# Weights loaded in one go, score banks apart in the first segment, and a planner with refitted transfers and a reserve on every engine, in an attention and Fourier kernel

## The chip, the cores and the metric

The kernel runs on one core of one Trainium2 chip. The core has TensorE (PE in the profile: matmuls; PEld: its weight loads), VectorE (DVE), ScalarE (ACT), GpSimd (POOL) and SyncE (SP), which here issues all the DMAs. The metric is the device time of one launch in microseconds. Three runs of the kernel before took 1836.32, 1828.71 and 1827.49 us; the median is 1828.71.

## The reference

Four layers on x of 2048 rows by 512: attention with a compressive memory (A), a two-dimensional Fourier transform (B), and both again with the same weights. Each is added to its input, after a layer norm.

```python
def _A_ref(x, wq, wk, wv, wo, beta):          # 32 heads of 16, N=4 segments of L=512
    q, k, v = heads(x @ wq), heads(x @ wk), heads(x @ wv)
    phi = lambda t: jnp.where(t > 0, t + 1.0, jnp.exp(t))
    for s in range(N):
        logits = einsum("bhqd,bhkd->bhqk", qs, ks) * scale + mask     # causal
        a_dot = einsum("bhqk,bhkd->bhqd", softmax(logits), vs)
        a_mem = einsum("bhld,bhde->bhle", phi(qs), M) / (einsum("bhld,bhd->bhl", phi(qs), z) + 1e-6)
        outs.append(g * a_mem + (1.0 - g) * a_dot)                    # g = sigmoid(beta)
        M = M + einsum("bhld,bhle->bhde", phi(ks), vs)
        z = z + phi(ks).sum(rows)
    return concat(outs) @ wo
def _B_ref(x, ...):                            # real part of the 2D transform
    a, b = x @ dft_hid_re.T, x @ dft_hid_im.T
    return dft_seq_re @ a - dft_seq_im @ b
x = x + _A_ref(_layernorm(x), ...); x = x + _B_ref(_layernorm(x), ...)   # and both once more
```

## The kernel before

Float32 products are made of float16 halves: every operand is scaled by a power of two and split into a high and a low half (`split`, L367), and three matmuls (`mm3`, L324) make one product.

**Streams.** The work is written as sixteen generators (L1071) and short tasks (`spawn`, L321). Each yields what it needs next: an engine, the tiles that it reads, and the kinds of buffers that it takes. The loop at L1079 asks the planner (`Plan`, L40) when each could go, takes the one with the earliest time, and lets it issue its next instructions. So the order of the instructions on each engine is fixed when the program is built, by the planner's estimates; at run time each engine works its list in that order, and waits where an operand is late. `Plan.op` (L135) holds the estimates: a duration for each operation, a latency after it (`LAT`, L43), and for a DMA the issue and a tail (L171 to L175, or an `est` at the call). `RESERVE` (L35) makes the loop count data that POOL or a DMA wrote as ready 500 or 1000 ns later, for TensorE alone (L132).

**Attention.** A segment of 512 rows has four groups of eight heads (eight segments in two layers, so 32 groups, numbered from 0). For each group: projections of q and k (`s_p`, L682; 24 matmuls, `b<-g,w` in the profile) and v (`s_v`, L707; 48, `b<-w,g`); the halves go through DRAM (`d`) into `qst` and `kst` (`t_split`, L584), of which there are two each (`NR`), so that group i+2 is loaded when the second pass of group i is done. A first pass of scores (`s_x`, L777; 32 matmuls `b<-kst,qst`) serves only to find each row's maximum: DVE adds the causal mask and reduces (`t_max`, `junk<-b,cmask`), the maxima are transposed on PE (`b<-identf,mx`) and written into two rows of `qst` by DMA. A second pass (`s_st`, L827; 32 matmuls `b<-qst,kst`) gives the transposed scores with the maximum taken off; ACT takes the exponential, POOL masks (`t_sel`, L816), and `s_av` (L849) multiplies with v (`b<-w,vt`). `s_mem` (L730) keeps the memory (`b<-vt,w` and `b<-w,macc`). `t_merge` (L548) divides, with the reciprocal of the sums going through DRAM and back.

**After it.** `s_o` (L904) multiplies with wo (`b<-wo,w`), `t_res` adds and takes the layer norm, `s_ab` (L1010) multiplies with the hidden transform (`b<-wd,w`), and `s_f` (L1041) with the sequence transform (`b<-w,w`, 3072 matmuls in 14 chunks), whose blocks are loaded raw, scaled and split once (`s_r`, `s_c`) and kept in DRAM for the second layer.

**Weights.** At the start (L273 to L285) the four tiles of x and the blocks of wq and wk for group 0 are loaded. `s_w` (L376) takes the largest magnitude of each block (`absmax`), finds the scale (`scales`, L348: a transpose on PE, a reduction, and a matmul with ones that spreads it), splits the block and stores it to DRAM for the later segments. After group 0's blocks it waits for the four layer norms, then loads the other ten blocks and `beta`, takes the scale of wv over all four blocks, and goes on group by group. `s_wo` (L415) does the same with wo and the hidden transform.

**Buffers.** Eight banks of PSUM (L255) are shared among four kinds, each with a number kept for it and a most: `pj` for projections and the like, `av`, `dft`, and `ss` for both passes of scores.

Of the kernel before, what the change touches and what calls it, by code (L numbers as in the profile page):

```python
# [31 lines left out]
SLACK = 0  # L32
# [7 lines left out]
class Plan:  # L40


    LAT = dict(T=197.0, V=150.0, A=165.0, G=100.0, Y=0.0)  # L43

    def __init__(self):
        self.free = dict.fromkeys("VGATYD", 0.0)
        self.acc = {}
        self.cols = {}
        self.wr = {}
        self.rd = {}  # L50
        self.area, self.count, self.slot = {}, {}, {}
        self.fresh = set()
        self.fine = {}
        self.by = {}
        self.dma = None
        self.mode, self.units, self.begun, self.entered = "m", {}, 0.0, 0.0
# [67 lines left out]
    def ready(self, reads, tags, eng):  # L124
# [3 lines left out]
        for t in reads:  # L128
# [3 lines left out]
            r = max(r, self.wr.get(n, 0.0) + (RESERVE.get(self.by.get(n), 0.0) if eng == "T" else 0.0))  # L132
        return r

    def op(self, eng, name, args, kw):  # L135
# [7 lines left out]
        if eng == "T":  # L143
            n, w = out[0].free_size(), aps[1]
            slow = 4 if w.dtype == F32 else 1
            c = n / 2.4 * slow + (18 if w.dtype == F32R else 3)
            cols = n * slow * w.partition_size() / 128
            mode, unit = "m", 0
            if name == "matmul" and out[0].partition_size() == 32:
                mode, unit = "v", out[0].start_partition() // 32  # L150
            elif w.partition_size() <= 64:
                mode, unit = "h", w.start_partition() // 64
        elif eng == "A":
# [11 lines left out]
        elif eng == "G":  # L165
            c = 127 + n * 0.915 if name == "affine_select" else 96 + n * 2.2
# [4 lines left out]
        else:  # L171
            stored = out[0].space == bass.MemoryType.DRAM
            c, tail = self.dma or (440, 350 if stored else 950)
            if kw.get("transpose"):
                c, tail = 1350, 450  # L175
# [25 lines left out]
        if eng == "T":  # L201
            self.begun = t
            self.units[unit] = e
            if len(self.units) < dict(m=1, h=2, v=4)[mode]:
# [39 lines left out]
def body(ctx: ExitStack, tc: tile.TileContext, x, wq, wk, wv, wo, beta, wd, cs, out):  # L244
# [10 lines left out]
    pl.setup(psum, "b", 8, dict(pj=(1, 4), av=(2, 2), dft=(1, 2), ss=(2, 4)))  # L255
    pl.setup(work, "w", NW, dict(
        xi=(4, 6), hl=(1, 4), qhl=(1, 3), phm=(2, 3), phr=(1, 2), mu=(1, 1), kt=(1, 2), pn=(1, 2), md=(2, 2), mz=(1, 1),
        en=(1, 1), wt=(2, 3), wv=(1, 2), craw=(4, 8), cc=(4, 8), pt=(8, 12), ot=(4, 8), xb=(2, 4),
# [26 lines left out]
    load(0, 1)  # L285
    macc = const.tile([128, NG, 2, 4, 32], F32, name="macc")
# [34 lines left out]
    def spawn(g):  # L321
        tasks.append([next(g, None), g])
# [8 lines left out]
    mk = const.tile([128, 1], F32, name="mk")  # L331
    V.memset(mk, 0.0)
# [15 lines left out]
    def scales(a, b):  # L348
        k = b - a
        yield need("T", amax[:, b - 1:b], tag="ss")  # L350
        pm = ps("ss")
        T.transpose(pm[0:k, 0:128], amax[:, a:b], identf)
        yield need("V", pm)
        V.tensor_reduce(mk[0:k], pm[0:k, 0:128], axis=AX.X, op=OP.max)
        V.tensor_scalar(mk[0:k], mk[0:k], 1e-30, None, op0=OP.max)
        dg = rg("dg", 3, F32, (128, 4))
        V.tensor_scalar(dg[:, 0:k], identf[:, 0:k], mk, None, op0=OP.mult)
        yield need("T", dg)
        T.matmul(pm[:, 256:256 + k], ones, dg[:, 0:k], start=True, stop=True)
        yield need("V", pm)  # L360
        gi, si, vi = (t[:, a:b].bitcast(I32) for t in (gmax, scl, inv))
        V.tensor_scalar(gi, pm[:, 256:256 + k].bitcast(I32), 0x7F800000, None, op0=OP.bitwise_and)
        pl.close(pm)
# [8 lines left out]

    def flat(t):
        return t.rearrange("p a b -> p (a b)")

    def s_w():  # L376
        def part(n, g):
# [3 lines left out]
            yield from split(w, stage[g][n], scl[:, i:i + 1])  # L381
# [5 lines left out]
        for g in range(NG):  # L387
            for n in range(2):
                yield need("V", stage[g][n])
                absmax(2 * g + n, flat(stage[g][n]))  # L390
            yield from scales(2 * g, 2 * g + 2)
            for f, n, e in ((f_q, 0, -10), (f_k, 1, -10), (f_k2, 1, 12)):
                V.tensor_scalar(f[g], inv[:, 2 * g + n:2 * g + n + 1], 2.0 ** e, None, op0=OP.mult)
            V.tensor_scalar(f_s[g], inv[:, 2 * g:2 * g + 1], inv[:, 2 * g + 1:2 * g + 2], 2.0 ** 22,
# [769 lines left out]
```

## Time and profile before

| | |
|---|---|
| median of three runs | 1828.71 us |
| span of the profiled execution | 1824.8 us |
| TensorE busy | 1697.8 us, 93% |
| VectorE busy | 1085.9 us, 60% |
| ScalarE busy | 897.1 us, 49% |
| GpSimd busy | 724.6 us, 40% |
| mean granted TensorE clock | 0.971 |
| DMA | 242.44 MB, 133 GB/s |

The page gives the span of the profiled execution, from its first instruction to its last; its time with what lies around the span isn't given apart from the runs, whose median is 3.9 us over the span. "Busy" leaves out waits. A row of the timeline has its start, its length, engine, line, operation, tiles written and read (buffer numbers left out), shapes and count, and in brackets the idle time ahead of it with what ended it. Since nearly all instructions are issued in one helper, they carry its line, L237, and are told apart by their tiles.

### The profile page before, as it was taken

How to read it: one execution, taken by the hardware profiler on the slowest of the kernel's cores; microseconds unless marked ns; L12 is line 12 of the kernel's file. 1: busy time of each engine (PE TensorE's matmuls, PEld its weight loads, DVE VectorE, ACT ScalarE, POOL GpSimd, SP SyncE). 2: the span in 40 equal slices, each digit the busy share in tenths (PEclk: the TensorE clock that was granted, in tenths of full speed). 3: DMA queues.
4: the chain of work that ended last, by engine and by line, in shares of the span. 5: the costliest groups of instructions: out<-in, count | busy, mean ns of one | idle time of the engine just before them, and what ended most of it. 6: DMA issues, size and time to landing. Idle time of an engine off the chain costs nothing. (4 is left out here: it accounts for less than half of the span.)

```text
span 1824.8 us, 32643 instructions
## 1 busy us (share of the span) xinstructions
PE 1697.8 (93%) x11045; PEld 742.2 (41%) x11045; DVE 1085.9 (60%) x3404; ACT 897.1 (49%) x1563; POOL 724.6 (40%) x1158
## 2 busy tenths in 40 slices
PE   3878799989989999999999879999999999999999
PEld 2433334443433434344444333434444434444444
DVE  7786955577765877565556655564656567533211
ACT  2557656757465666644436655555445444431000
POOL 3234545546363464553434543442534334231000
PEclk8988899999999999999999898999999999999999
DMA  7345535655454653345784541553544444222233
GB/s 190 105 135 132 170 74 165 156 152 150 127 147 136 191 149 102 119 151 167 232 226 156 136 124 49 144 131 100 132 110 114 141 120 102 83 84 81 93 122 115
DMA packets 240985, 242.44 MB, mean 133 GB/s; under 512 B 129777, under 2 KB 152305, under 8 KB 240817
## 3 DMA queue, kind: packets, MB, share of 16 engines
q1 hardware_dynamic: 240816, 240.35, 46.9%
q8 instruction: 87, 1.43, 0.3%
q14 instruction: 82, 0.66, 0.1%
HBM read 152.96 MB, written 63.70 MB: 119 GB/s over the span
## 5 line engine op out<-in xcount | busy, mean ns | idle before, releaser
L237 PEld LDWEIGHTS <-w 128*128 128x128 f16 x4992 | 463.8, 98 | 613.3 <-issue 113.0
L237 PE MATMUL b<-w,w 128*128 128x512 f16 x3072 | 708.9, 380 | 2.0 <-ACT w L237 1.7
L237 POOL TENSOR_TENSOR w<-w,w 128x512 f16<-128x512 f32 (+1 forms) x316 | 380.6, 1208 | 412.6 <-ACT w L237 266.9
L237 ACT ACTIVATE w<-b,fac 128x512 f32<-128x512 f32 (+1 forms) x728 | 420.9, 658 | 176.6 <-PE b L237 156.0
L237 DVE CUSTOM_DVE_ANT_0 junk<-b,cmask 128x128 bf16<-128x128 f32 (+3 forms) x1024 | 437.6, 485 | 77.7 <-PE b L237 76.3
L237 POOL TENSOR_SCALAR_AFFINE_SELECT w<-w 128x128 f32<-128x128 f32 (+2 forms) x704 | 242.4, 357 | 309.5 <-ACT w L237 302.6
L237 DVE SCALAR_TENSOR_TENSOR y<-b,fyu,y 128x512 f32<-128x512 f32 x200 | 149.2, 746 | 217.7 <-PE b L237 217.2
L237 ACT ACTIVATE w<-b 128x512 f32<-128x512 f32 (+1 forms) x240 | 138.2, 600 | 251.9 <-PE b L237 240.4
L237 ACT ACTIVATE w<-w,csc 128x512 f16<-128x512 f32 (+1 forms) x256 | 181.1, 721 | 60.7 <-DVE csc L237 51.5
L237 PE MATMUL b<-g,w 128*128 128x512 f16 x768 | 190.4, 391 | 7.4 <-DMA g<-w 5.8
L237 PE MATMUL b<-w,vt 128*32 128x512 f32 (+3 forms) x2048 | 186.2, 460 | 3.0 <-POOL w L237 2.2
L237 PE MATMUL b<-wd,w 128*128 128x512 f16 x768 | 178.7, 380 | 0.9 <-DVE w L237 0.5
L237 ACT ACTIVATE w<-w 128x512 f16<-128x512 f32 (+1 forms) x144 | 90.7, 635 | 168.5 <-DVE w L237 117.4
L237 DVE SCALAR_TENSOR_TENSOR w<-b,w 128x512 f16<-128x512 f32 x128 | 88.1, 688 | 132.6 <-ACT w L237 131.9
L237 PE MATMUL b<-kst,qst 62*128 62x128 f16 (+3 forms) x1024 | 131.9, 314 | 25.3 <-DMA kst<-d 10.0
L237 PE MATMUL b<-qst,kst 64*128 64x512 f16 (+3 forms) x1024 | 123.8, 308 | 16.4 <-ACT w L237 6.1
L237 PE MATMUL b<-w,g 128*128 128x128 f16 x1536 | 99.5, 224 | 10.9 <-DVE mx L237 4.8
L237 PEld LDWEIGHTS <-g 128*128 128x128 f16 x1536 | 91.2, 100 | 25.1 <-issue 14.5
L237 PEld LDWEIGHTS b<-w,vt 128*32 128x32 f32 x2048 | 55.9, 111 | 101.0 <-issue 56.4
L237 PEld LDWEIGHTS <-kst 64*128 64x128 f16 x1024 | 38.3, 95 | 137.2 <-issue 124.7
L237 PE MATMUL b<-wo,w 128*128 128x512 f16 x384 | 89.7, 379 | 0.2 <-ACT w L237 0.2
L237 DVE DVE_READ_ACCUMULATOR2_ANT mx<- 128x1 f32 x1024 | 84.5, 83 | 0.0
(102 smaller groups left out, 887.1 us busy)
## 6 DMA issues: line engine op xcount, KB each, us to landing
w<-in_cs_dram SPq DMA_DIRECT2D x128, 256.0 KB
cc<-w SPq DMA_DIRECT2D x128, 256.0 KB
w<-cc SPq DMA_DIRECT2D x128, 256.0 KB
w<-w SPq DMA_DIRECT2D x96, 256.0 KB
d<-w SPq DMA_DIRECT2D x128, 128.0 KB
w<-rec SPq DMA_DIRECT2D x56, 256.0 KB
w<-in_x_dram SPq DMA_DIRECT2D x32, 256.0 KB
qst<-d SPq DMA_DIRECT2D x64, 128.0 KB
```

The lines of the kernel that those rows point to most:

```text
L237: r = f(*args, **kw)
```

## The change

**Loads.** All twelve blocks of wq, wk and wv, and `beta`, are loaded at the start, straight after x. The pools of split blocks may hold up to eight and four.

**Scales.** `scales` is one matmul with ones over the partitions' maxima, so the sum of 128 maxima stands in for the largest, and the scale is smaller by some powers of two. `s_w` takes the scale of group 0's blocks first, then the maxima of all the others and one matmul for seven columns. `share` takes the place of `split` for all blocks but group 0's wq and wk: ACT writes the high half, and then the scaled block in place; POOL or DVE (`tt` chooses) subtracts.

**Banks.** Until the first output projection (`together`) the first pass has banks of the kind `sx`, the second of `st`, two to four each; then both share `ss` as before.

**Planner.** Latencies, the time of small matmuls in float32 and of 32-row ones, POOL's time and all DMA estimates have new values; a DMA has an issue, a time on the queue and a tail, and SP is held while eight are under way. The reserve holds for every engine. The rule that holds back scores while other matmuls are ready now takes in whatever takes a score bank, the transpose of the maxima too. `RANK` is empty, so it only replaces the way to choose among equals.

```diff
-SLACK = 0
+RANK = {}
+APART = dict(pj=(1, 4), av=(1, 2), dft=(0, 2), sx=(2, 4), st=(2, 4), ss=(0, 4))
+SHARED = dict(pj=(1, 4), av=(2, 2), dft=(1, 2), sx=(0, 2), st=(0, 2), ss=(2, 4))
...
-    LAT = dict(T=197.0, V=150.0, A=165.0, G=100.0, Y=0.0)
+    LAT = dict(T=235.0, V=115.0, A=150.0, G=85.0, Y=25.0)
...
-            r = max(r, self.wr.get(n, 0.0) + (RESERVE.get(self.by.get(n), 0.0) if eng == "T" else 0.0))
+            r = max(r, self.wr.get(n, 0.0) + RESERVE.get(self.by.get(n), 0.0))
...
-            c, tail = self.dma or (440, 350 if stored else 950)
+            c, took, tail = self.dma or ((415, 917, 364) if stored else (470, 829, 755))
...
+        if eng == "Y" and len(self.lands) >= 8:
+            t = max(t, self.lands[-8])
...
-            self.free["D"] = max(self.free["D"], e + 650) + out[0].nbytes() / 360
+            self.free["D"] = max(self.free["D"], e + 590) + took
             e = self.free["D"] + tail
+            self.lands.append(e)
...
-    pl.setup(psum, "b", 8, dict(pj=(1, 4), av=(2, 2), dft=(1, 2), ss=(2, 4)))
+    pl.setup(psum, "b", 8, dict(APART))
...
     load(0, 0)
     load(0, 1)
+    Y.dma_start(gb[:, 0, :], beta)
+    for j in range(NG):
+        for n in range(3):
+            if j or n == 2:
+                load(j, n)
...
     def scales(a, b):
         k = b - a
-        yield need("T", amax[:, b - 1:b], tag="ss")
-        pm = ps("ss")
-        T.transpose(pm[0:k, 0:128], amax[:, a:b], identf)
+        yield need("T", amax[:, b - 1:b], tag="dft")
+        pm = ps("dft")
+        T.matmul(pm[:, :k], ones, amax[:, a:b], start=True, stop=True)
         yield need("V", pm)
-        V.tensor_reduce(mk[0:k], pm[0:k, 0:128], axis=AX.X, op=OP.max)
-        V.tensor_scalar(mk[0:k], mk[0:k], 1e-30, None, op0=OP.max)
-        dg = rg("dg", 3, F32, (128, 4))
-        V.tensor_scalar(dg[:, 0:k], identf[:, 0:k], mk, None, op0=OP.mult)
-        yield need("T", dg)
-        T.matmul(pm[:, 256:256 + k], ones, dg[:, 0:k], start=True, stop=True)
-        yield need("V", pm)
+        V.tensor_scalar(gmax[:, a:b], pm[:, :k], 1e-30, None, op0=OP.max)
+        pl.close(pm)
...
+    def share(o, src, s):
+        yield need("A", src, s)
+        A.activation(o[:, 0], src, AF.Copy, scale=s)
+        A.activation(src, src, AF.Copy, scale=s)
+        yield need("VG", o, src)
+        tt(o[:, 1], src, o[:, 0], OP.subtract)
...
+        yield from scales(0, 2)
+        yield from part(0, 0, split)
+        yield from part(1, 0, split)
+        for j in range(1, NG):
             for n in range(2):
+                yield need("V", stage[j][n])
+                absmax(2 * j + n, flat(stage[j][n]))
+        for j in range(NG):
+            yield need("V", stage[j][2])
+            V.tensor_reduce(vm[:, j:j + 1], flat(stage[j][2]), axis=AX.X, op=OP.max,
+                            apply_absolute_value=True)
+        V.tensor_reduce(amax[:, 8:9], vm, axis=AX.X, op=OP.max)
+        yield from scales(2, 9)
+        factors(0, NG)
+        done.add("WL")
+        yield from part(2, 0, share)
+        for g in range(1, NG):
+            for n in range(3):
+                yield from part(n, g, share)
...
+    def together():
+        apart[0] = False
+        kinds.update(SHARED)
...
-                if w[2][:2] == ("ss", "ss") and r + EARLY >= other:
-                    both = pl.ready(w[1], w[2] + ("ss", "ss"), w[0])
+                if w[2][:1] in (("ss",), ("sx",), ("st",)) and r + EARLY >= other:
+                    both = pl.ready(w[1], w[2] + w[2][:2], w[0])
```

**What moves.** SyncE's list near the program's start, before: `y` is where the weights land, `g` the transposed x, `w_128` a block stored to DRAM.

```order
L237 DMA y<-in_wk_dram 128x4x128
L237 DMA_TRANSPOSE g_276<-w_305 128x8x128
L237 DMA_TRANSPOSE g_276<-w_308 128x8x128
L237 DMA_TRANSPOSE g_276<-w_316 128x8x128
L237 DMA_TRANSPOSE g_276<-w_345 128x8x128
L237 DMA w_128<-w_344 128x1024
L237 DMA w_129<-w_354 128x1024
L237 DMA gb<-in_beta_dram 128x4
L237 DMA y<-in_wv_dram 128x4x128 x2
```

The same place on SyncE with the change:

```order
L246 DMA y<-in_wq_dram 128x4x128
L246 DMA y<-in_wk_dram 128x4x128
L246 DMA y<-in_wv_dram 128x4x128
L246 DMA_TRANSPOSE g_285<-w_316 128x8x128
L246 DMA_TRANSPOSE g_285<-w_323 128x8x128
L246 DMA_TRANSPOSE g_285<-w_329 128x8x128
L246 DMA w_137<-w_342 128x1024
L246 DMA w_138<-w_355 128x1024
L246 DMA_TRANSPOSE g_285<-w_350 128x8x128
L246 DMA y<-in_wo_dram 128x4x512
```

The ten loads that stood behind the transposes and the stores stand ahead of them, and the fourth transpose stands behind two stores.

TensorE's list where group 0's first pass ends and its maxima are transposed, before: `w_580` is group 1's block of wq.

```order
L237 MATMUL b_664<-kst_102,qst_104 128x512
L237 LDWEIGHTS qst_104
L237 MATMUL b_665<-kst_102,qst_104 128x512
L237 MATMUL b_675<-identf,mx 32x128
L237 LDWEIGHTS w_580
L237 MATMUL b_683<-g_276,w_580 128x512
```

With the change `w_773` is a block of group 3, and `kst_114` and `qst_116` hold group 1:

```order
L246 MATMUL b_875<-g_285,w_773 128x512
L246 MATMUL b_889<-identf,mx 32x128
L246 LDWEIGHTS w_773
...
L246 LDWEIGHTS qst_116
L246 MATMUL b_912<-kst_114,qst_116 128x128
...
L246 MATMUL b_913<-kst_114,qst_116 128x128
```

Projections of all four groups stand ahead of this place or at it, and group 1's first pass follows at once; before, group 1's projections came here, and its first pass after group 0's second.

TensorE's list at the end of group 1's first pass, with the change; `qst_115` and `kst_113` hold group 0:

```order
L246 MATMUL b_1011<-kst_114,qst_116 128x512
L246 LDWEIGHTS kst_113
L246 MATMUL b_1018<-qst_115,kst_113 128x512
...
L246 MATMUL b_1026<-qst_115,kst_113 128x512
L246 LDWEIGHTS qst_116
L246 MATMUL b_1031<-kst_114,qst_116 128x512
```

Group 0's second pass stands between the pairs of group 1's first, in banks of its own.

More of the change, by code (lines that the diff above doesn't have):

```diff
@@ L1112, in body @@
         if ready:
-            first = min(r for r, _ in ready)
-            best = next(q for q in ready if q[0] <= first + SLACK)
+            best = min(ready, key=lambda q: (q[0], q[1][2]))
         if best is None:
```

110 lines of the change are left out of this document (52 added, 58 removed).

## The prediction

> **What bounds the kernel now.** I read the page first, for the engine that is nearest to full, then the windows, to see in which stretches it is not full, then TensorE's timeline at the start.
>
> ```profile
> span 1824.8 us, 32643 instructions
> PE 1697.8 (93%) x11045; PEld 742.2 (41%) x11045; DVE 1085.9 (60%) x3404; ACT 897.1 (49%) x1563; POOL 724.6 (40%) x1158
> PE   3878799989989999999999879999999999999999
> PEclk8988899999999999999999898999999999999999
> ```
>
> TensorE (PE) is busy 93% of the span, no other engine over 60%. The slices show where the rest lies: the first six or so, and a dip about slice 23. So an edit can only win PE's idle time, 1824.8 - 1697.8 = 127.0 us, and what a lowered clock costs beside it.
>
> ```profile
> 0.00:266.00 266.00, 201.25 (x1421) 88.08 (x1423) 202.31 (x718) 136.98 (x243) 98.99 (x181) 0.88 0.49 136
> 266.00:1000.00 734.00, 707.39 (x4555) 315.49 (x4552) 472.02 (x1392) 433.70 (x730) 361.11 (x503) 0.99 0.55 157
> 1000.00:1110.00 110.00, 91.79 (x692) 36.72 (x692) 69.84 (x274) 63.78 (x116) 46.38 (x98) 0.86 0.47 126
> 1110.00:1825.00 715.00, 697.37 (x4382) 301.95 (x4378) 341.69 (x1022) 262.67 (x474) 218.08 (x377) 1.00 0.39 108
> ```
>
> The columns are the stretch, its length, busy time of PE, its weight loads, DVE, ACT and POOL, then the granted PE clock and the DMAs. PE idles 64.8 us in the first 266 us (266.00 - 201.25), at a clock of 0.88; 26.6 in the next 734; 18.2 about the second layer's start; 17.6 in the last 715. I cut at 266 because the first matmul of the sequence transform comes there; from then on PE always has transform work to put between the steps of the attention. What comes before is a chain of steps, and the change works on that chain.
>
> ```profile
> 18.87 8.23 PE L237 MATMUL b<-g,w 128*128 128x512 f16 x24 [5.79 <-DMA g<-w]
> 30.41 0.27 PE L237 MATMUL b<-identf,amax 128*1 128x128 f32 x1 [3.31 <-DVE amax L237]
> 36.54 0.27 PE L237 MATMUL b<-w,g 128*128 128x128 f16 x1 [4.02 <-ACT w L237]
> ...
> 40.98 0.61 PE L237 MATMUL b<-kst,qst 62*128 62x128 f16 x8
> ...
> 55.80 0.39 PE L237 MATMUL b<-identf,mx 128*32 128x128 f32 x1 [3.91 <-DVE mx L237]
> 55.99 4.19 PE L237 MATMUL b<-g,w 128*128 128x512 f16 x12
> ...
> 62.30 0.60 PE L237 MATMUL b<-qst,kst 64*128 64x512 f16 x4
> ...
> 80.73 0.62 PE L237 MATMUL b<-kst,qst 62*128 62x128 f16 x12
> ...
> 96.49 0.40 PE L237 MATMUL b<-identf,mx 128*32 128x128 f32 x1 [1.62 <-DVE mx L237]
> ...
> 128.83 0.28 PE L237 MATMUL b<-identf,mx 128*32 128x128 f32 x1 [2.78 <-DVE mx L237]
> ...
> 162.18 0.27 PE L237 MATMUL b<-identf,mx 128*32 128x128 f32 x1
> ...
> 229.81 3.40 PE L237 MATMUL b<-wo,w 128*128 128x512 f16 x15 [0.15 <-ACT w L237]
> ...
> 266.29 1.90 PE L237 MATMUL b<-w,w 128*128 128x512 f16 x8
> ```
>
> Each row has its start and length, and in brackets the wait and what ended it. Group 0's projections run at 18.87, its scores (kst,qst) at 40.98, the transpose of its maxima (mx) at 55.80, its second pass (qst,kst) at 62.30. Group 1's projections come only now, at 55.99, since its weights were loaded late; so its scores begin at 80.73. Maxima of groups 1, 2 and 3 are transposed at 96.49, 128.83 and 162.18. The output projection (wo) starts at 229.81, the first transform at 266.29.
>
> **The change part by part.** *Weights at once.* All twelve blocks are loaded behind x, so SyncE's queue has 16 loads of 256 KB, 4.19 MB, ahead of the transposes that PE first needs.
>
> ```profile
> 24.00:27.00 3.00, 3.00 (x13) 1.12 (x11) 0.92 (x2) 0.60 (x1) 0.00 (x0) 1.00 1.17 316
> 9.35 7.59 SPq L237 DMA_TRANSPOSE g<-w  x4
> ...
> 21.36 0.51 SPq L237 DMA_DIRECT2D y<-in_wv_dram  x1
> ...
> 32.01 1.94 SPq L237 DMA_DIRECT2D qst<-d  x4
> 33.99 1.81 SPq L237 DMA_DIRECT2D kst<-d  x4
> ```
>
> ```profile
> 26.77 0.69 DVE L237 TENSOR_REDUCE vm<-y 128x1 f32<-128x512 f32 x1 [1.26 <-DMA y<-in_wv_dram]
> ```
>
> At the 316 GB/s of the window 4.19 MB take 13.3 us, so they land at 15 to 18 us. The order then has three transposes, two stores and the fourth transpose. In the trace a load issued at 21.36 behind others was used at 26.77, 5.4 us later, so I count waiting in the queue: projections at 22.5 and not 18.87, +3.6. Its ends are 0 (the four transposes are issued from 9.35 to 16.94 now, by when the loads may be over) and +8. The Trainium skill, "DMA: Bandwidth & Descriptors", Queues, rings and completion order, says that each DMA engine takes descriptors in ring order, which speaks against this edit. By it the +3.6 stands; without it the sum would be 3.6 us better. The trace shows it for loads behind loads, and no row shows a transpose behind twelve.
>
> *One matmul for each scale, of seven columns.* It takes two reductions, a transpose and a matmul away; the waits of 3.31 and 4.02 us at 30.41 and 36.54 shrink, since V's block is known to be there. With it group 1's projections and V's of group 0 are put ahead of group 0's scores, into time in which PE idled. From the end of group 0's projections (18.87 + 8.23 = 27.1) to its scores (40.98) it is 13.9 us of splits and copies through DRAM, which stay: scores at 22.5 + 8.6 + 14 = 45, 4 us later.
>
> ```profile
> L237 DVE CUSTOM_DVE_ANT_0 junk<-b,cmask 128x128 bf16<-128x128 f32 (+3 forms) x1024 | 437.6, 485 | 77.7 <-PE b L237 76.3
> L237 DVE DVE_READ_ACCUMULATOR2_ANT mx<- 128x1 f32 x1024 | 84.5, 83 | 0.0
> L237 ACT ACTIVATE w<-b,fac 128x512 f32<-128x512 f32 (+1 forms) x728 | 420.9, 658 | 176.6 <-PE b L237 156.0
> L237 ACT ACTIVATE w<-b 128x512 f32<-128x512 f32 (+1 forms) x240 | 138.2, 600 | 251.9 <-PE b L237 240.4
> L237 DVE SCALAR_TENSOR_TENSOR w<-b,w 128x512 f16<-128x512 f32 x128 | 88.1, 688 | 132.6 <-ACT w L237 131.9
> ```
>
> *Score banks apart.* Maxima of one group take DVE (437.6 + 84.5) / 32 = 16.3 us at most; exponentials take ACT 22 x 0.658 = 14.5 us, and have a pair of banks of their own. Group 0's maxima: 14.8 us now (40.98 to 55.80), plus five splits of projections at 0.688 and a memory update that DVE now does beside them, 4.2 us: done at 45 + 14.8 + 4.2 = 64. Group 1's scores follow at once: done at 64 + 17 = 81, and not 96.5. Group 2 needs the buffers of group 0, which its second pass frees at 64 + 6.5 (from 55.80 to 62.30 now) + 14.5 + 3 of other activations = 88, and 7 us of reloading (the issues take 1.94 and 1.81, and the last has to land): 95 + 16 = 111, not 128.8. Group 3 in the same way, with four us of weight splits on ACT: 138, not 162.2. Now it is 229.81 - 162.18 = 67.6 us from there to wo, and 36.5 more to the transform; I take 63 and 33, since fewer matmuls stand between: wo at 201, the transform at 234, 32 us earlier.
>
> *What is given back.* Fewer matmuls stand ahead of the first transform in the changed order: 144 of the projections and not 180, 288 of V's and not 336, 192 scores and not 216, 20 memory updates and not 24.
>
> ```profile
> L237 PE MATMUL b<-g,w 128*128 128x512 f16 x768 | 190.4, 391 | 7.4 <-DMA g<-w 5.8 <-ACT w L237 1.2 <-DVE w L237 0.4
> L237 PE MATMUL b<-w,g 128*128 128x128 f16 x1536 | 99.5, 224 | 10.9 <-DVE mx L237 4.8 <-ACT w L237 4.0 <-DVE w L237 1.4
> L237 PE MATMUL b<-kst,qst 62*128 62x128 f16 (+3 forms) x1024 | 131.9, 314 | 25.3 <-DMA kst<-d 10.0 <-DVE mx L237 6.3 <-ACT w L237 5.0
> L237 PE MATMUL b<-vt,w 128*128 128x192 f32 x192 | 42.7, 363 | 6.5 <-POOL w L237 3.1 <-ACT vt L237 1.8 <-issue 1.5
> ```
>
> Busy time over count gives 36 x 0.248 + 48 x 0.065 + 24 x 0.129 + 4 x 0.445 (two passes each) = 16.9 us, and with ten scale matmuls and two of the memory some 19. So the transform has to come before 266 - 19 = 247 for anything to be won, and 234 wins **13 us**. Its ends are 0, where each step is as late as now, and 30, where DVE alone sets the steps (45 + 4 x 17 = 113 for the last maxima, less what ACT and the buffers hold).
>
> *Splits moved to ACT and POOL (share).*
>
> ```profile
> L237 DVE SCALAR_TENSOR_TENSOR w<-y,scl,w 128x512 f16<-128x512 f32 x12 | 8.9, 738 | 0.3 <-ACT w L237 0.3
> L237 ACT ACTIVATE w<-y,scl 128x512 f16<-128x512 f32 x12 | 8.5, 723 | 9.1 <-DVE scl L237 9.1
> ```
>
> 22 splits leave DVE at 0.738 us, 16 us, and put a second activation on ACT, at 0.723, 16 us. They lie beside the exponentials of groups 1 to 3 and are in the steps above; if that cover is gone they are a rival, below.
>
> *Estimates and the reserve.* They take no instruction away, but shift the order in all the rest. After 266 the idle time is 26.6 + 18.2 + 17.6 = 62.4 us. I have no row that prices a new order: between a third of it saved and a third added, 20 us either way, I take **2 us** saved, nearest to nothing, because the distance from maxima to the second pass grows in some groups and shrinks in others. About the second layer's start, the 18.2 us, the order is nearly the same as now.
>
> *The clock.*
>
> ```profile
> 95.00:125.00 30.00, 25.20 (x208) 10.71 (x208) 25.57 (x91) 18.57 (x34) 11.12 (x25) 0.92 0.56 170
> 125.00:151.00 26.00, 16.96 (x93) 5.14 (x93) 19.08 (x79) 15.34 (x27) 14.26 (x29) 0.67 0.39 102
> ```
>
> The granted clock falls to 0.67 in a stretch whose longest wait is the 2.78 us at 128.83. The Trainium skill, "TensorE: Matmul & The Clock Gate", Part 1, has the clock go down after an idle window of about 3.4 us; here less is enough, and the measurement decides. By the rule only the three long waits at the start would cost clock, by the row the short ones of groups 1 to 3 too; I count no gain from it, and by the row it could be 3 us.
>
> The sum: 1824.8 - 13 - 2 = 1809.8 us of span; the median of the runs is 1828.71, 3.9 above the profiled span, so 1813.7, and with 1 to 2 us for the clock **1812**.
>
> **The rivals.** *The later order gains too*: if the estimates fit, waits after 266 fall by a third, 20 us: 1792, and with the upper end at the start 1780. For it speaks that all the waits there are short; against it that PE is at 96% there already. *The head start is given back*: the transform comes at about 247, because the fourth transpose and the seven-column matmul, behind which PE's queue waits for twelve loads, cost their upper ends, or the new order adds a third to the waits: 1828. *ACT takes DVE's place*: the shares put 12 pairs of activations among the exponentials of groups 1 to 3, and ACT, which waits 156 us for PE there, cannot make them up. Its work is 88 exponentials at 0.658, 24 activations at 0.723 and some 26 copies at 0.600, 91 us or 22.7 a group; in my steps they begin at 71 and end at 168, 66 us ahead of the transform. At 27.5 us a group the transform comes at 71 + 110 + 66 = 247, and nothing is won: that is the point. At 32 it comes at 265, with 19 us of work put behind it: 1846, slower. Against it: ACT is busy 137 of the first 266 us. *The change doesn't do what it says*: the wider weight pool (up to eight) could take buffers from the transform's, but the order never holds more than three, so I give it no chance.
>
> **How the numbers follow.** The forecast, 1800 to 1819, 0.47. The later gain too, 1780 to 1800, 0.18. Given back, 1820 to 1838, 0.21. ACT in the way, 1838 to 1860, 0.14. About 0.5%, 9.1 us, is what a measurement of this kernel can tell from no change; so faster (below 1819.6) 0.65, within 0.21, slower (over 1837.9) 0.14. The range is 1788 to 1838: it leaves out the slower rival, and the lowest third of the better one.
>
> **What would show it.** Right: group 0's scores near 45 us, the four transposes of maxima near 64, 81, 111 and 138, wo near 201 and the first transform near 234, with PE's idle time after it near 60 us. Wrong: projections later than 26 us (the queue), a matmul with seven columns with a wait of over 2 us ahead of it, exponentials back to back on ACT through groups 1 to 3 with PE waiting for ACT, or idle time after the first transform outside 40 to 80 us.

## The result, and the profile after

Four runs of the changed kernel took 1779.09 to 1781.48 us, median 1780.26; four of the kernel before, beside them, 1825.83 to 1836.32, median 1828.1. The ratio is 0.9729, with a 95% interval of 0.9707 to 0.975: 2.7% faster, and below the predicted range of 1788 to 1838. Of the page of the changed kernel, the rows that answer to those of before:

```profile
span 1778.3 us, 32593 instructions
...
PE 1682.4 (95%) x11032; PEld 735.8 (41%) x11032; DVE 1060.6 (60%) x3357; ACT 915.4 (51%) x1585; POOL 744.2 (42%) x1178
```

The span is 46.5 us shorter. TensorE's idle time fell from 127.0 to 95.9 us (1778.3 - 1682.4), its busy time by 15.4. Where the idle time went, the windows say. They are cut at each kernel's first matmul of the sequence transform; first the kernel before, then the changed one (columns as in the prediction):

```profile
0.00:266.30 266.30, 201.55 (x1424) 88.10 (x1425) 202.52 (x719) 137.00 (x244) 98.99 (x181) 0.88 0.49 136
266.30:1824.80 1558.50, 1496.26 (x9624) 654.14 (x9622) 883.35 (x2685) 760.14 (x1320) 625.57 (x977) 0.99 0.47 132
```

```profile
0.00:237.00 237.00, 177.63 (x1291) 77.03 (x1292) 169.01 (x611) 145.42 (x253) 116.90 (x197) 0.89 0.54 141
237.00:1778.30 1541.30, 1504.74 (x9744) 658.76 (x9742) 891.64 (x2746) 770.00 (x1333) 627.25 (x981) 0.99 0.49 136
```

Length less busy time: ahead of the first transform 64.8 us idle before and 59.4 after, 5.4 less; behind it 62.2 before and 36.6 after, **25.7 less**. Of the 15.4 us of busy time, 3.6 are the matmuls of the scales (groups of 2.1 and 3.1 us gave way to one of 1.6). The other 11.8 are about what the clock can give: (1 - 0.971) x 1824.8 = 52.9 us lost to it before, (1 - 0.977) x 1778.3 = 40.9 after, 12.0 less, half of it ahead of the transform (0.12 x 266.3 = 32.0, and 0.11 x 237 = 26.1). That is an upper estimate, since the mean clock counts idle time too.

The steps of the start, in TensorE's timeline of the changed kernel:

```profile
23.56 4.40 PE L246 MATMUL b<-g,w 128*128 128x512 f16 x12 [12.05 <-DMA g<-w]
27.80 0.28 PE L246 MATMUL b<-amax,ones 128*128 128x7 f32 x2
...
45.15 0.62 PE L246 MATMUL b<-kst,qst 62*128 62x128 f16 x12
...
62.33 0.28 PE L246 MATMUL b<-identf,mx 128*32 128x128 f32 x1
82.14 0.28 PE L246 MATMUL b<-identf,mx 128*32 128x128 f32 x1
111.19 0.28 PE L246 MATMUL b<-identf,mx 128*32 128x128 f32 x1 [1.18 <-DVE mx L246]
138.05 0.28 PE L246 MATMUL b<-identf,mx 128*32 128x128 f32 x1 [0.40 <-DVE mx L246]
...
207.51 1.46 PE L246 MATMUL b<-wo,w 128*128 128x512 f16 x6
...
236.97 2.12 PE L246 MATMUL b<-w,w 128*128 128x512 f16 x9
```

They are nearly those of the forecast: projections at 23.56 (22.5), scores at 45.15 (45), maxima transposed at 62, 82, 111 and 138 (64, 81, 111, 138), wo at 207.5 (201), the transform at 237.0 (234). What was not foreseen lies behind the last row.

Which waits went there, the groups of TensorE's instructions from 267 us on show; before, then after (busy time and mean ns, then the idle time ahead of the group and what ended it):

```profile
L237 PE MATMUL b<-kst,qst 62*128 62x512 f16 (+3 forms) x808 | 100.0, 312 | 19.2 <-DMA kst<-d 9.4 <-ACT w L237 4.3 <-DVE mx L237 3.1
...
L237 PE MATMUL b<-w,g 128*128 128x128 f16 x1200 | 76.7, 223 | 5.5 <-DVE mx L237 4.8 <-DMA w<-w 0.7
...
L237 PE MATMUL b<-identf,mx 128*32 128x128 f32 x26 | 7.3, 281 | 11.4 <-DVE mx L237 11.4
```

```profile
L246 PE MATMUL b<-kst,qst 62*128 62x512 f16 (+3 forms) x832 | 97.5, 306 | 4.6 <-DVE mx L246 2.6 <-ACT w L246 0.7 <-DMA qst<-mhl 0.4
...
L246 PE MATMUL b<-w,g 128*128 128x128 f16 x1238 | 76.0, 219 | 0.0
...
L246 PE MATMUL b<-identf,mx 128*32 128x128 f32 x26 | 7.3, 279 | 7.6 <-DVE mx L246 6.3 <-ACT w L246 1.3
```

First passes (kst,qst) waited 19.2 us and now 4.6; the 9.4 us for the transfer kst<-d, seven waits, are gone. Ahead of the longest of them stands a queue. In SyncE's timeline of the kernel before, and then TensorE's:

```profile
1064.30 0.65 SPq L237 DMA_DIRECT2D w<-rec  x1
1065.00 1.16 SPq L237 DMA_DIRECT2D w<-w  x2
1066.26 1.07 SPq L237 DMA_DIRECT2D den<-w  x2
1067.42 1.77 SPq L237 DMA_DIRECT2D kst<-d  x4
```

```profile
1071.81 0.26 PE L237 MATMUL b<-kst,qst 62*128 62x128 f16 x1 [3.91 <-DMA kst<-d]
```

The last piece of kst is issued by 1069.19, behind a broadcast, two loads of blocks and two small stores, and PE can go on at 1071.81; by then it has stood still for 3.9 us, since the order put the pass here.

### The profile page after: what moved, and what is told of

Same layout as the page of the kernel before. It is cut to its first block, busy times and chain, and to the rows that moved or that the text cites. A ratio compares the mean times of both kernels' runs of the same rounds, so it can differ in the third digit from the quotient of the medians.

```text
span 1778.3 us, 32593 instructions
## 1 busy us (share of the span) xinstructions
PE 1682.4 (95%) x11032; PEld 735.8 (41%) x11032; DVE 1060.6 (60%) x3357; ACT 915.4 (51%) x1585; POOL 744.2 (42%) x1178
## 4 chain that ended last, share of the span: by engine, by line
PE 79%; DVE 6%; DMA 4%; issue 4%; ACT 4%; POOL 2%; SPq 1%; ACTq 0%; POOLq 0%; DVEq 0%
PE b L246 79%; ACT w L246 3%; DVE junk L246 2%; DMA w<-w 2%; POOL w L246 1%; DVE w L246 1%; SPq L246 1%; DVE cam L246 1%; DVE y L246 1%; DVE mx L246 0%; DMA g<-w 0%; DVE bst L246 0%; DMA qst<-d 0%; DMA d<-w 0%; DMA cc<-w 0%
## 5 line engine op out<-in xcount | busy, mean ns | idle before, releaser
L246 POOL TENSOR_TENSOR w<-w,w 128x512 f16<-128x512 f32 (+1 forms) x314 | 376.8, 1205 | 409.3 <-ACT w L246 278.4
L246 PE MATMUL b<-g,w 128*128 128x512 f16 x768 | 185.5, 386 | 16.9 <-DMA g<-w 12.8
L246 PE MATMUL b<-w,vt 128*32 128x512 f32 (+3 forms) x2048 | 178.8, 457 | 0.7 <-POOL w L246 0.5
L246 PE MATMUL b<-qst,kst 64*128 64x512 f16 (+3 forms) x1024 | 130.0, 308 | 12.4 <-ACT w L246 4.3
L246 PE MATMUL b<-kst,qst 62*128 62x128 f16 (+3 forms) x1024 | 130.7, 312 | 11.6 <-DVE mx L246 6.9
```

Source lines behind the costliest of these rows:

```text
L246: r = f(*args, **kw)
```

## The experiments

Each row is one kernel: the median of its runs; its first transform; PE's idle time ahead of it and behind it, and the mean granted clock, all of the profiled execution (idle is length less busy time of windows cut as above). The clock of one execution is a rough figure: 24 of the kernel before, run beside a8_split, have 0.964 to 0.972. The kernel before ran beside all of them, at medians of 1824.6 to 1826.5.

| kernel | median us | first transform | idle ahead | idle behind | clock |
|---|---|---|---|---|---|
| before | 1828.1 | 266.3 | 64.8 | 62.2 | 0.971 |
| b3_lat_pe | 1838.1 | 276.2 | 77.3 | 54.0 | 0.970 |
| b4_lat_act | 1825.8 | 271.6 | 69.7 | 57.6 | 0.965 |
| b5_broadcast | 1823.2 | 274.9 | 65.7 | 51.6 | 0.965 |
| b2_transfers | 1801.6 | 266.5 | 68.2 | 37.9 | 0.973 |
| b6_no_hold | 1807.2 | 265.5 | 66.2 | 44.0 | 0.972 |
| b1_planner | 1800.7 | 272.9 | 70.3 | 36.1 | 0.967 |
| after | 1780.3 | 237.0 | 59.4 | 36.6 | 0.977 |
| p1_lat_pe | 1788.2 | 240.7 | 58.0 | 41.0 | 0.971 |
| p2_lat_act | 1793.3 | 244.7 | 65.6 | 41.9 | 0.971 |
| a1_reserve_pe | 1801.4 | 253.6 | 66.9 | 39.2 | 0.971 |
| a2_old_estimates | 1800.1 | 246.6 | 63.6 | 49.9 | 0.973 |
| a3_old_planner | 1798.0 | 239.6 | 60.6 | 51.3 | 0.975 |
| d1_old_transfers | 1815.7 | 249.6 | 66.0 | 53.1 | 0.972 |
| d2_old_latencies | 1795.6 | 253.0 | 67.6 | 38.0 | 0.971 |
| a4_banks_shared | 1784.2 | 246.4 | 62.1 | 35.5 | 0.972 |
| a5_old_weights | 1803.7 | 247.7 | 60.6 | 41.8 | 0.966 |
| a8_split | 1793.5 | 252.4 | 66.5 | 37.7 | 0.968 |
| c1_late_loads | 1785.6 | 245.9 | 62.4 | 36.7 | 0.970 |
| c2_apart_twice | 1785.5 | 239.2 | 59.1 | 35.8 | 0.972 |

**The planner and the rest.** First the planner's part alone on the kernel before (b1_planner: the new estimates, the reserve, the hold on scores and the choice among equals), and the rest alone (a3_old_planner). The edit that makes a3 of the changed kernel, cut:

```diff
-    LAT = dict(T=235.0, V=115.0, A=150.0, G=85.0, Y=25.0)
+    LAT = dict(T=197.0, V=150.0, A=165.0, G=100.0, Y=0.0)
...
-            r = max(r, self.wr.get(n, 0.0) + RESERVE.get(self.by.get(n), 0.0))
+            r = max(r, self.wr.get(n, 0.0) + (RESERVE.get(self.by.get(n), 0.0) if eng == "T" else 0.0))
...
-            c, took, tail = self.dma or ((415, 917, 364) if stored else (470, 829, 755))
+            c, tail = self.dma or (440, 350 if stored else 950)
...
-                if w[2][:1] in (("ss",), ("sx",), ("st",)) and r + EARLY >= other:
+                if w[2][:2] in (("ss", "ss"), ("sx", "sx"), ("st", "st")) and r + EARLY >= other:
```

> The kernel before with the planner's part of the change alone (estimates, reserve, hold); loads, scales, splits, banks and pools as before. If the planner took the later idle time: 1795 to 1802, the first transform near 266 us, idle time behind it near 37 us. If the early start handed it on: 1822 to 1832. If new orders scatter: anything between, not the complement of the run with the old planner.

> The changed kernel with the planner of before: old estimates, the reserve for TensorE alone, and the hold for pairs of score banks alone. Loads, scales, share, banks and pools stay changed. If the planner (reserve or estimates) took the later idle time: 1806 to 1815, the first transform still before 245 us, idle time behind it near 60 us. If the early start handed it on: 1778 to 1788.

The ratios are 0.9865 (0.9831 to 0.99) and 0.9837 (0.9799 to 0.9875): half and some 60% of the gain. In b1 it lies behind the first transform, where PE idles 36.1 us. In a3 the transform comes early (239.6), but that alone is not the gain: of the 27.1 us by which its span is shorter, 4.2 are idle time ahead of the transform, 10.9 idle time behind it, and 12.0 busy time. Behind the transform 51.3 us are left, where near 60 was expected.

**Reserve or estimates.** Of the diff above, a1 takes only the second piece, a2 only the estimates (and the hold of SP at eight under way), both on the changed kernel.

> The changed kernel, with the reserve counted for TensorE alone as before. What is to be found is where 26 us of TensorE's idle time behind the first transform went (62.4 us before, 36.5 with the change). If the reserve on the other engines took it: idle time there back near 60 us and the time near 1806. If the refitted estimates took it, or the start handed it on: 1778 to 1786, idle time near 37. If any new order of this program scatters by 10 to 20 us: somewhere between, without a match elsewhere.

> The changed kernel with all estimates of before (latencies, small matmuls, POOL, DMA issue and tail, no hold at eight DMAs); the reserve holds on every engine. If the estimates took the later idle time: near 1806, idle time behind the first transform near 60 us. If the reserve took it: 1778 to 1786. The start should keep its head start in either case, the first transform at 230 to 245 us.

Without the reserve the idle time behind the first transform stays low (39.2), with the old estimates it is 49.9, not the 60 of the expectation but clearly more: there it is the estimates. In total both lose about 20 us (0.9864 and 0.9858), a1 at the start, where its transform comes 16.6 us later. Whether the reserve does that, or any new order would, the next pair tells.

**How far orders scatter.** One estimate moved by 5 ns, in the changed kernel (p1, p2) and in the one before (b3, b4):

```diff
-    LAT = dict(T=235.0, V=115.0, A=150.0, G=85.0, Y=25.0)
+    LAT = dict(T=240.0, V=115.0, A=150.0, G=85.0, Y=25.0)
```

> The changed kernel with one estimate moved by 5 ns (latency after a TensorE operation 240 and not 235), to see how far a new order scatters by itself. Scatter (any new order lands within 10 to 20 us, and 1780 was a lucky one): 1787 to 1802, the idle time after the first transform back at 45 to 60 us. Estimates are causes (a small step of an estimate keeps what they won): 1777 to 1785, idle time after the first transform 33 to 41 us.

> The changed kernel with the latency after a ScalarE operation 155 and not 150 ns, a second draw of the same kind. Scatter: 1787 to 1802. Estimates are causes: 1777 to 1785. If one of the two draws stays and the other goes, the scatter is about half of the 20 us that single parts of the change showed, and differences under 10 us are not to be put down to a part.

> The kernel before with the latency after a TensorE operation 202 and not 197 ns, a draw of another order around the old estimates. If the old estimates of DMAs cause the idle time: 48 to 62 us of it after the first transform, and 1805 to 1835. If the kernel before was an unlucky draw and the estimates cause little: 36 to 45 us, 1795 to 1805.

> The kernel before with the latency after a ScalarE operation 170 and not 165 ns, a second draw. Old estimates as a cause: 48 to 62 us idle after the first transform, 1805 to 1835. Unlucky draw: 36 to 45 us, 1795 to 1805.

The changed kernel's three orders take 1780.3, 1788.2 and 1793.3 us, those of the one before 1825.8, 1828.1 and 1838.1. So a total says nothing of a part under some 13 us, and the changed kernel is the best of its three: against their means, 1787.3 and 1830.7, the change is worth 43 us, not 48. Idle time behind the first transform scatters less, 36.6 to 41.9 and 54.0 to 62.2, and the two sets stay apart. It is the better yardstick, and the kernel before was no odd one. In p1 and p2 the total came out nearer to what scatter would give, and the idle time to what the estimates as a cause would give.

**Which estimates.** All of the DMAs' go back in d1, all others in d2, on the changed kernel; b2 has the DMAs' alone on the kernel before, b6 has them without the hold of SP at eight under way, b5 only the broadcast's. In the new numbers nearly every transfer, taken alone, lands within half a microsecond of where the old ones had it, but most hold the queue longer: a piece of kst 0.52 us where its size gave 0.18 or 0.36, the broadcast 1.909 us where it was 0.728. From b2's edit, cut (the `est` of single transfers change too):

```diff
-            c, tail = self.dma or (440, 350 if stored else 950)
+            c, took, tail = self.dma or ((415, 917, 364) if stored else (470, 829, 755))
+            took *= out[0].nbytes() / 262144 if self.dma is None else 1
...
+        if eng == "Y" and len(self.lands) >= 8:
+            t = max(t, self.lands[-8])
...
-            self.free["D"] = max(self.free["D"], e + 650) + out[0].nbytes() / 360
+            self.free["D"] = max(self.free["D"], e + 590) + took
```

> The changed kernel with the old estimates of all DMAs (and without the hold at eight under way); latencies and PE times stay new. If the transfers' estimates made the gain after the first transform, it comes out like the kernel with all old estimates: 1795 to 1802, idle time after the first transform 46 to 52 us, with waits for kst<-d back near 10 us. If the latencies made it, 1780 to 1786 with 36 to 40 us idle there.

> The changed kernel with the old latencies, PE and POOL times; the DMA estimates stay new. If the transfers' estimates made the gain, 1780 to 1786, idle time after the first transform 36 to 40 us and kst<-d waits under 2 us; if the latencies made it, 1795 to 1802 and 46 to 52 us.

> The kernel before with the new estimates of DMAs alone (and the hold at eight under way). So far six kernels with the new estimates of DMAs idle 36.1 to 41.9 us on PE after the first transform, four with the old ones 49.9 to 62.3. If those estimates alone make that difference: idle time after the first transform 36 to 43 us, kst<-d waits under 3 us, first transform at 262 to 275 as before, and 1800 to 1812 in all. If they need the new latencies or the reserve beside them: 50 us or more idle there, and 1815 to 1830.

> The kernel before with the new estimates of DMAs but without the hold at eight under way. If the times of the transfers make the gain: idle time after the first transform 36 to 43 us, waits for kst<-d under 3 us, 1798 to 1812. If the hold makes it: 50 to 62 us idle there, waits for kst<-d near 5 to 10 us, 1815 to 1838.

> The kernel before with one transfer's estimate renewed: the broadcast of the reciprocals (w<-rec, 256 KB written, 56 of them) holds the queue for 1.909 us in the planner and not 0.728, with the same end for itself. Before, PE waits up to 3.9 us for kst<-d, issued behind such a broadcast. If this one estimate makes the gain: waits for kst<-d under 3 us, idle time after the first transform 36 to 43 us, 1798 to 1808. If the gain is spread over all transfers or lies in the hold at eight: 48 to 62 us, 1810 to 1835.

The windows behind the first transform, of d1, d2 and b2:

```profile
249.60:1813.50 1563.90, 1510.81 (x9752) 658.69 (x9750) 893.99 (x2743) 768.76 (x1334) 621.08 (x985) 0.99 0.48 132
```

```profile
253.00:1793.30 1540.30, 1502.28 (x9746) 658.93 (x9744) 895.90 (x2748) 767.27 (x1329) 624.85 (x978) 0.99 0.49 135
```

```profile
266.50:1802.00 1535.50, 1497.64 (x9636) 653.93 (x9634) 884.73 (x2689) 763.16 (x1323) 623.63 (x976) 0.99 0.48 135
```

Idle: 53.1, 38.0 and 37.9 us. For d1 and d2 that is what the transfers as the cause would give, or a microsecond over it; their totals lie outside what was expected, 1815.7 (1795 to 1802) and 1795.6 (1780 to 1786). And the waits for kst<-d, which were to come back to near 10 us in d1, did not:

```profile
L241 PE MATMUL b<-kst,qst 62*128 62x384 f16 (+3 forms) x812 | 101.9, 306 | 10.3 <-DVE mx L241 3.8 <-ACT w L241 3.8 <-DMA kst<-d 0.7
```

From 267 us on, PE waits there for maxima (DVE mx) 16.0 us in all and for POOL's w 12.9, where the changed kernel has 10.9 and 4.9. So the swap of the transfers' estimates is what moves the idle time, and waits for kst<-d are where it shows in the kernel before (9.4), b3 (6.9), b4 (7.7), b5 (4.8) and a2 (5.9), but not in a3 (1.4) and d1.

b2 is the plainest run of the study: nothing but numbers for DMAs and the hold, the transform where it was (266.5), and the time is 0.9872 (0.9852 to 0.9892) of before. Of its groups from 267 us on:

```profile
L242 PE MATMUL b<-kst,qst 62*128 62x512 f16 (+3 forms) x808 | 99.8, 305 | 5.8 <-ACT w L242 2.6 <-DVE mx L242 2.0 <-DVE y L242 0.3
...
L242 PE MATMUL b<-w,g 128*128 128x128 f16 x1200 | 75.2, 219 | 0.0
...
L242 PE MATMUL b<-identf,mx 128*32 128x128 f32 x26 | 7.4, 285 | 2.8 <-DVE mx L242 2.8
```

The wait for kst<-d is gone, as in the changed kernel, and of the waits for maxima, 11.4 and 4.8 us before, 2.8 and nothing are left (7.6 and nothing in the changed kernel). That those were passed on from late first passes is argued, not shown. What the hold adds lies within the scatter: without it 44.0 us idle and 1807.2 (0.9891, 0.9867 to 0.9915), a microsecond over what I had set for "the times make the gain" and far from 50. The broadcast's estimate alone leaves 51.6 us, and its ratio, 0.9982 (0.9962 to 1.0003), is no gain: the expectation that it is the one fell. In all, every kernel with the new times of DMAs idles 35.5 to 44.0 us there (13 kernels), every one without them, or with the broadcast's alone, 49.9 to 62.2 (7).

**Banks and weights.** a4 has the banks shared from the start, a5 the old loads, scales and splits:

```diff
-    pl.setup(psum, "b", 8, dict(APART))
+    pl.setup(psum, "b", 8, dict(pj=(1, 4), av=(2, 2), dft=(1, 2), ss=(2, 4)))
...
-                    yield need("T", qs, ks, tag=(kx, kx), mode="h")
+                    yield need("T", qs, ks, tag=("ss", "ss"), mode="h")
```

```diff
-    for j in range(NG):
-        for n in range(3):
-            if j or n == 2:
-                load(j, n)
...
+        yield need("T", amax[:, b - 1:b], tag="ss")
+        pm = ps("ss")
+        T.transpose(pm[0:k, 0:128], amax[:, a:b], identf)
...
-        yield from part(2, 0, share)
-        for g in range(1, NG):
-            for n in range(3):
+        for g in range(NG):
```

> The changed kernel with the score banks shared from the start, as before the change. If the banks carry the early start (first passes beside second passes): transposes of maxima of groups 2 and 3 move back from 111 and 138 to 120 to 129 and 150 to 162, the first transform comes 10 us or more later than in the kernels with banks apart (237 to 254). If the weights carry it: 62, 82, 111 to 115 and 138 to 145, first transform 237 to 254. Idle time after the first transform stays at 36 to 43 us either way.

> The changed kernel with the old loads, scales and splits of the weights; banks stay apart and the planner new. If the weights carry the early start: projections at about 19 us, maxima of group 0 transposed near 56 to 64, of group 1 near 96 and not 82, the following near 128 and 160, first transform near 266 to 273. If the banks carry it: maxima of groups 2 and 3 at 111 to 118 and 138 to 146, and the first transform at 237 to 254. Idle time after the first transform stays at 36 to 43 us either way.

Transposes of the maxima of groups 1 and 2, in a4 and then in a5:

```profile
90.39 0.28 PE L246 MATMUL b<-identf,mx 128*32 128x128 f32 x1 [0.61 <-DVE mx L246]
120.15 0.36 PE L246 MATMUL b<-identf,mx 128*32 128x128 f32 x1 [1.37 <-DVE mx L246]
```

```profile
79.84 0.39 PE L246 MATMUL b<-identf,mx 128*32 128x128 f32 x1
112.25 0.40 PE L246 MATMUL b<-identf,mx 128*32 128x128 f32 x1
```

With shared banks these maxima are 8 to 9 us late, half of the way back to b1 (98.5 and 130.7), which has neither; with the old weights and the banks apart they are on time. So here the banks are enough, and without them the weights win about half. The totals go the other way. Without the banks it is 1784.2, within the scatter of the changed kernel; without the weights 1803.7, no better than b1 with neither. So the early maxima alone are worth nothing that shows. What the weights are worth is not settled as a mechanism: of the 26.4 us by which a5's span is longer than that of the changed kernel, only 6.5 are idle time and 3.7 scale matmuls (3.2 + 2.1 - 1.6); 16.2 are more busy time in the same matmuls (1702.3 - 1682.4 - 3.7), at a mean clock of 0.966 against 0.977. That execution was the slowest of a5's four; the other three have 0.970 to 0.971, and by the medians a5 is still 23.4 us slower.

**The splits.** Only `share` falls away, for wo and the hidden transform too (cut):

```diff
-                yield from part(n, g, share)
+                yield from part(n, g, split)
```

> The changed kernel with the old way to split (ACT and DVE) for all blocks of weights, wo and the hidden transform, so that only the new way falls away. If ScalarE is in the way with the new one (my rival): exponentials of groups 1 to 3 start earlier, maxima of group 3 before 138, first transform before 237, 1770 to 1778. If DVE gains by it: maxima of groups 1 to 3 later by 2 to 6 us, first transform 240 to 255, 1782 to 1795. If neither matters: 62, 82, 111, 138 within 2 us and a total in the scatter, 1777 to 1795.

Group 1's maxima stay at 82.5, those of groups 2 and 3 come at 118.8 and 144.9 and not 111.2 and 138.1, the transform at 252.4. ScalarE is not in the way, since nothing comes earlier without `share`. That DVE gains by it is likely and not shown: 118.8 is later than in any kernel with the banks apart and `share`, but a1, which has `share`, comes to 145.0 for group 3 and 253.6 for the transform. The total, 1793.5, is at the end of the scatter, so its worth is open.

**The queue of loads.** Six blocks go behind the transposes, and wv gets a scale matmul of its own (cut):

```diff
-        for n in range(3):
-            if j or n == 2:
-                load(j, n)
+        load(j, 2)
...
+        yield gate(*[("L", 0, t) for t in range(TT)])
+        for j in range(1, NG):
+            load(j, 0)
+            load(j, 1)
```

> The changed kernel with the six blocks of wq and wk of groups 1 to 3 loaded behind the transposes of x; the four of wv stay ahead, with a scale of their own. If the queue of twelve loads holds back the projections (23.56 and not 18.87): they start at 19 to 21 us and group 0's scores at 41 to 43. The total then moves by what the start hands on, 4 us at most, inside the scatter: 1774 to 1795. If the queue is not what holds them back: projections at 23 to 24 us as now.

TensorE's timeline, then SyncE's:

```profile
20.27 0.59 PE L246 MATMUL b<-amax,ones 128*128 128x1 f32 x2 [8.49 <-DVE amax L246]
20.71 7.57 PE L246 MATMUL b<-g,w 128*128 128x512 f16 x24
...
45.76 0.61 PE L246 MATMUL b<-kst,qst 62*128 62x128 f16 x12
```

```profile
34.71 4.48 SPq L246 DMA_DIRECT2D w<-w  x4
39.28 2.32 SPq L246 DMA_DIRECT2D kst<-d  x4
```

The loads did hold the projections back: 20.71 and not 23.56. What ends PE's wait now is the maximum for that extra scale matmul, so the transposes had landed by then. But group 0's scores are no earlier (45.76 and 45.15). Four stores of weights now stand ahead of kst in the same queue, whose loads are issued at 39.28 and not, as in the changed kernel, at 37.21; PE comes to the scores from other matmuls in both, without a wait for kst, so that the stores are the reason is argued, not shown. SyncE in the changed kernel, at the last transpose of x and at kst:

```profile
19.74 1.29 SPq L246 DMA_TRANSPOSE g<-w  x1
...
36.69 0.42 SPq L246 DMA_DIRECT2D w<-w  x1
37.21 1.78 SPq L246 DMA_DIRECT2D kst<-d  x4
```

**The second layer's start.** Banks apart there as well:

```diff
+                if q == NSEG and t == 0:
+                    apart[0] = True
+                    kinds.update(APART)
...
-            if not q:
+            if s == 0:
                 together()
```

> The changed kernel with score banks apart in the first segment of the second layer too. There PE idles 21.8 us and has 23.9 us at a lowered clock. If shared banks cause that, it falls to 10 to 14 us idle there and the whole to 1765 to 1775. If the chain through x, layer norm and transposes causes it (nothing else ready), it stays at 20 to 24 us idle there, and the whole lies in the scatter that two 5 ns steps showed, 1777 to 1795.

The windows about the second layer's start, of the changed kernel and of this one:

```profile
877.60:1086.80 209.20, 187.42 (x1372) 82.02 (x1371) 134.45 (x503) 118.32 (x207) 87.77 (x154) 0.94 0.55 151
```

```profile
879.80:1084.50 204.70, 185.50 (x1328) 80.86 (x1328) 131.77 (x497) 113.63 (x197) 83.77 (x146) 0.92 0.55 150
```

21.8 us idle, and 19.2 with banks apart, not the 10 to 14 that shared banks as the cause would give: what PE waits for there is hardly the banks. The total, 1785.5, lies in the scatter. No kernel of the study beats the changed one.

## Why the prediction was wrong

**Projections, scores, maxima, transform.** Right, within 3 us but for wo (6.5 late). The 3.6 us for the loads ahead of the transposes measured 4.7, and 1.8 are left in c1, with six loads moved. The rows put most of it into the issue: the last transpose is issued by 21.03 (19.74 + 1.29) and before by 16.94, 4.1 us later, and from there to the first projection it is 2.5 us and not 1.9. The Trainium skill, "DMA: Bandwidth & Descriptors", Queues, rings and completion order, has each DMA engine take descriptors in ring order; no run here shows that by itself.

**Head start, 13 us.** Right in size only if the clock is counted in: 5.4 us of idle time and 3.6 of scale matmuls make 9, and with some 6 of clock ahead of the transform, which I had as a term of its own, 15. PE's busy time ahead of the transform fell by 23.9 us; less scales and clock, some 14 of them were put behind it, where I put 19, scale matmuls among them, which do not move but go. The cause was only half right: the steps were those of the banks, as I had it, but a4 shows that the total does not need them.

**Estimates and the reserve, 2 us.** This step failed: "They take no instruction away, but shift the order in all the rest. [...] I take **2 us** saved, nearest to nothing, because the distance from maxima to the second pass grows in some groups and shrinks in others." The stretch that it speaks of lost 25.7 us of idle time, and about 6 of clock. The estimates of the DMAs are the greater part: b2 changes those numbers and the hold alone and takes 24.3 us (62.2 - 37.9) of idle time out of that stretch; on the changed kernel the swap gives 11.9 (a2 to d2) and 16.5 (d1 to after). I looked at the order, where a shift may go either way, and not at what ends the waits: the row of first passes, 25.3 us with kst<-d 10.0 ahead, stood in the prediction, and it is a row that prices late transfers. It is not the whole price, since d1 idles 53.1 us with 0.7 of them. The bound of 20 us was too near as well, and the sign set for a wrong forecast, idle time outside 40 to 80 us, came up with 36.6.

**The clock, 1 to 2 us.** Too low: up to 12. The prediction has no working for its figure, and the rows beside it are of the start alone; half of the 12 lies behind the first transform.

**From span to median, 3.9 us.** It set the median against the span of another execution. Where a run has both, they lie 1.7 to 2.0 us apart, so this term was 2 us too large.

Of the 32 us between 1812 and 1780.3, the idle time behind the transform has 24, the clock some 10, the last term 2; the head start, without the clock, gives 4 back.

**The rivals.** "The later order gains too", at 0.18, is what happened: it had a third of 62.4 us, and 41% went (25.7 of 62.2). "Given back" and "ACT takes DVE's place" did not happen; maxima and transform came on time, and a8 speaks for `share`. The case that I had at 0.47 did not happen. The two neighbours, 1788.2 and 1793.3, lie inside the range, the 1780.3 of this order does not; some of the distance is the luck of an order, but the neighbours' idle time, 41.0 and 41.9 us, is not the 60 of the forecast either.

**Open.** Which of the DMAs' times it is (the broadcast's alone is not enough), and through which waits they act in the changed kernel; whether the reserve is worth anything (a1 is 8 us beyond the scatter, while b1, which has it, equals b2, which has not); why a5 is slower.

## What to carry to other kernels

Where a planner sets the order, read what ends the waits of the bounding engine: waits for transfers are a sign of wrong estimates, and correcting these can take away more idle time than those waits have, in places where the row names another engine. Before a part of such a change gets credit for ten microseconds, move one estimate by 5 ns and see how far the total goes by itself; a stretch's idle time is a steadier measure than the total. An earlier step wins nothing by itself: in c1 the projections came 2.9 us earlier and the scores no earlier, so read what stands ahead of the next step too, on the queue and on the engine.

## What the hardware showed unexpectedly

The mean granted clock lay between 0.965 and 0.977 over these twenty kernels, and PE's busy time for nearly the same matmuls between 1682.4 us (the changed kernel, 0.977) and 1705.0 (b5_broadcast, 0.965): 22 us, 3.6 of them scale matmuls, as much as most parts of the change. Each is one execution, and one order scatters too: 24 executions of the kernel before have 0.964 to 0.972. Between the changed kernel and p1_lat_pe, 5 ns apart in one estimate, the clock went from 0.977 to 0.971 and busy time from 1682.4 to 1687.4, 5.0 of the 8.1 us between their spans. All of it lies ahead of the first transform (177.6 and 182.7 us busy, at 0.89 and 0.86), where p1 idles 1.4 us less; behind it both are busy 1504.7 us. So the sum of the idle time alone does not set the clock. No run tells which idle stretches cost the clock.
